# A bound sent ahead of Q's relays, deferred products ahead of the weighting passes, and Q features due earlier in a fused attention and gated-MLP kernel

## The chip, the cores and the metric

One core of a Trainium2 chip runs the whole kernel in one launch. The metric is the device time of one execution in microseconds (us); lower is better. Engines are named as in the profile: PE is TensorE's matmul row, PEld its weight loads, DVE is VectorE, ACT is ScalarE, POOL is GpSimd, SP is SyncE, which here only issues DMAs. PSUM is the accumulator memory that PE writes.

## The reference

`xn` is the layer norm of `x` (2048 rows of 640). Two branches read it, and their results are combined:

```python
xn = _layernorm(x)
s = attention(xn)                       # below
g = silu((sigmoid(xn @ w_gate) * (xn @ w_up)) @ w_down)      # inner width 1536
out = x + s * g

# attention: 32 heads of 20, four segments of 512 rows, q/k/v = xn @ wq/wk/wv
for s in range(4):
    p = softmax(qs @ ks.T * scale + causal_mask)
    a_dot = p @ vs
    pq = phi(qs)                        # phi(t) = t+1 if t > 0 else exp(t)
    a_mem = (pq @ M) / (pq @ z + 1e-6)
    o = sigmoid(beta) * a_mem + (1 - sigmoid(beta)) * a_dot
    M, z = M + phi(ks).T @ vs, z + sum(phi(ks))
s = concat(o) @ wo
```

So each segment of 512 rows does causal softmax attention within itself, and reads a running memory `M` of the segments before it through the features `phi(q)`.

## The kernel before, in words

**Slots.** After a prologue the program is written out as 80 slots, 20 in each of the four segments. A slot handles one unit of the causal scores: four heads at a time, five units to a pair of head groups, four pairs to a segment. Slot `s` begins with `scores` (L516): four or eight groups of small matmuls into the one PSUM tile `Sps` (L522), then one 2048-wide exponential on ACT into `pt` (L527), then the causal cut on POOL (L530). One or two slots later `weigh` (L534) multiplies `pt` with V into the PSUM tile `Aps` (L547). When a head group is complete (after unit 2's first part and unit 4), `weigh` also puts three DVE instructions in line: the reciprocal `rd` (L553), its scaling (L554) and the product `od` (L556). `Aps` is single-buffered, so the next head group's first `weigh` waits for that `od`.

**What fills the slots.** All other work is put between `scores` calls by a planner. Its pieces are the next segment's projections (`v_tile` L360, `k_chunk` L289, `q_chunk` L321), the MLP (`gate` L428, `up` L438, `down` L456), the output projection (`o_proj` L502), the memory's update and reading (`m_update` L388, `mem_read` L410), loads and stores. `at(time, cost, ...)` gives a piece a due time in slots; the constant `R` = 20/24 scales the times in the text, so that `R * 18.3` is 15.25 slots after the segment's start. There are three heaps: `tasks` (PE work with a cost), `soft` (everything without), and `first` (only `phi`). The MLP's pieces stand in a list `bulk`, taken at a rate that evens out the slots' planned PE cost: a slot that has less fixed cost gets more of `bulk`. Within a slot the order is: `scores`; `fill` with `tasks` due before the slot's 0.45; the due `weigh` calls; `flush`; `phi` pieces due in this slot; `fill` with everything else due in it. `later(lag, ...)` puts the next step of a piece `lag * R` slots on.

**Deferred products.** `up` and `down` end in a DVE product (`hT` L442, `aa` L461) that frees one of only three PSUM buffers of the pool `d`, which all projections, MLP pieces and the bound share. The first part of each slot runs with `delay[0] = True`: these products are then kept in `pending` and issued by the `flush` behind the `weigh` calls, or sooner if the buffer is needed.

**Q, its bound and its features.** The scores need, beside Q, a bound on each score row so that the exponentials stay in range. Q's projection `q_chunk(n, c)` (five chunks) is copied to `q5`, with absolute values in `aq` (L324). `q_bound` (L329) multiplies `aq` with per-head column maxima of K (`cps`, L334), and ACT copies it to `cb` (L337). Q and bound then go out to DRAM and come back in the layout of `scores`, all through SP's one queue: `stage_out` writes `q5` (`Qs`, L310), `relay` reads it back as four DMAs (`QT<-Qs`, L274), `c_out` writes `cb` (`Cs`, L345), `c_in` reads it back as four DMAs per half into other rows of the same tiles (`QT<-Cs`, L353). Each half has its own `QT` tile. SP issues in program order and stops at a DMA whose wait isn't over.

`phi(n, "q5", c)` later overwrites `q5` with the features: an exponential on ACT into one of three `ex` buffers (L370; `cb` takes its buffer from the same three), and 0.8 R later two DVE instructions `rest` (L373, L374) in place, which must wait until the DMA to `Qs` has read the chunk. Only `mem_read` of the next segment's slots reads them.

**Prologue.** For segment 0 the same steps are written out by hand in `startup`. Behind Q's last chunk come `relay(0, 0, Qs, QT)`, `q_bound(0)`, the second half of Q, `c_in(0, (0,))`, then the loads of the second third of the MLP weights (`load_glu(1, 0)` and `(1, 1)`, L163: `Wg1`, `Wu1`), and the transposing DMAs of segment 1's `xn` (L263). PE meanwhile runs the eight first MLP pieces (`take`), then slot 0.

Of the kernel before, what the change touches and what calls it, by code (L numbers as in the profile page):

```python
# [55 lines left out]
R = NSLOT / 24  # L56
# [3 lines left out]
def kernel(  # L60
# [42 lines left out]
    def at(time, cost, fn, *a):  # L103
        count[0] += 1
        heapq.heappush(first if fn is phi else tasks if cost > 0.1 else soft, (time, count[0], cost, fn, a))
# [4 lines left out]
    def flush(keep=0):  # L110
        while len(pending) > keep:
            pending.pop(0)[1]()

    def dtile(shape, dtype, name):
        seq[0] += 1
        while pending and pending[0][0] <= seq[0] - 3:
            pending.pop(0)[1]()
        return ps_d.tile(shape, dtype, name=name, tag="d")
# [6 lines left out]
    def later(lag, fn, *a):  # L125
        at(clock[0] + lag * R, 0.0, fn, *a)
# [65 lines left out]
    def v_ones(a, b):  # L192
        for i in range(a, b):
            nc.gpsimd.memset(V[i][:, :, DH:VW], 1.0)
# [73 lines left out]
    def half_tile(tiles, n, half):  # L268
        return tiles[(2 * n + half) % 3]

    def relay(n, half, src, dst):
        rows = src[n % 2].rearrange("(g r d) n -> r d g n", r=4, d=DH)
        for r in range(4):
            nc.sync.dma_start(half_tile(dst, n, half)[32 * r:32 * r + DH, :, :], rows[r][:, 4 * half:4 * half + 4, :])  # L274
# [54 lines left out]
    def q_bound(n):  # L329
        s = st[n]  # L330
        ps = dtile([P, L], F32, "cps")
        for c in range(DC):
            b = c % 4
            nc.tensor.matmul(ps[32 * b:32 * b + H, :], lhsT=s["IK"][:, c, :], rhs=s["aq"][:, c, :],  # L334
                             start=(c < 4), stop=(c not in (0,)), tile_position=(0, 32 * b))
        cb = stg.tile([P, L], BF, name="cb", tag="ex", bufs=3)
        nc.scalar.copy(cb[:], ps[:])  # L337

        if n:
            later(0.8, c_out, n, cb)  # L340
        else:
            c_out(n, cb)

    def c_out(n, cb):
        nc.sync.dma_start(Cs[n % 2].rearrange("b h n -> (b h) n"), cb[:])  # L345
        if n:
            later(1.0, c_in, n)
# [215 lines left out]
    def take(k):  # L563
        for _, fn, a in bulk[:k]:
            fn(*a)
        del bulk[:k]
# [6 lines left out]
    def startup():  # L573
        warm(WARM)
        nc.gpsimd.memset(KT[0][:], 1.0)
        ln_stats(0, 0, 0, 1)
        ln_stats(0, 0, 1, 2)
        ln_norm(0, 0, 0)
        warm(10)
        ln_stats(0, 1, 0, 1)  # L580
        ln_norm(0, 0, 1)
        v_tile(0, 0, 0)
        ln_stats(0, 1, 1, 2)
        v_tile(0, 1, 0)
        ln_norm(0, 1, 0)
        v_tile(0, 0, 1)
        ln_norm(0, 1, 1)
        v_tile(0, 2, 0)
        v_tile(0, 1, 1)
        v_tile(0, 2, 1)  # L590
        v_ones(0, 4)
        make_ind()
        nc.gpsimd.memset(KT[1][:], 1.0)
        for c in range(DC):
            k_chunk(0, c)
        nc.gpsimd.memset(KT[2][:], 1.0)
        stage_out(0, 0, Ks, KT, "k5")
        for c in range(DC):
            q_chunk(0, c)
            if c == 0:  # L600
                stage_out(0, 1, Ks, KT, "k5")
                relay(0, 0, Ks, KT)
            elif c == 2:
                stage_out(0, 0, Qs, QT, "q5")
            if c < 2:
                ln_stats(1, 0, c, c + 1)
        make_bd()
        v_ones(4, 8)
        take(1)
        relay(0, 0, Qs, QT)  # L610
        q_bound(0)
        stage_out(0, 1, Qs, QT, "q5")
        c_in(0, (0,))
        load_glu(1, 0)
        load_glu(1, 1)
        ln_stats(1, 1, 0, 1)
        gates()
        take(1)
        ln_norm(1, 0, 0)
        ln_norm(1, 0, 1)  # L620
        take(1)
        ln_stats(1, 1, 1, 2)
        take(5)
        at(0.1, 0.68, v_tile, 0, 3, 0)
        at(0.5, 0.68, v_tile, 0, 3, 1)
        at(R * 2.0, 0.0, ln_norm, 1, 1, 0)
        at(R * 2.3, 0.0, ln_norm, 1, 1, 1)
        load_glu(2, 0)
        load_glu(2, 1)
        relay(0, 1, Ks, KT)  # L630
        relay(0, 1, Qs, QT)
        c_in(0, (1,))
# [6 lines left out]
    for n in range(NSEG):  # L639
        w = NSLOT * n  # L640
        m = n + 1
        if m < NSEG:
            if n:
                for p in range(2):
                    for i in range(2):
                        at(w + R * (1.4 * p + 0.7 * i - 3.4), 0.1, ln_stats, m, p, i, i + 1)
                        at(w + R * (0.4 + 1.6 * p + 0.4 * i), 0.1, ln_norm, m, p, i)
            for i in range(8):
                at(w + R * (3.5 + (0.6 * i if i < 4 else 2.5 + 0.55 * (i - 4))), 0.68, v_tile, m, i // 2, i % 2)
            for c in range(DC):  # L650
                at(w + R * (8.8 + 1.0 * c), 1.08, k_chunk, m, c)
                at(w + R * (13.8 + 1.1 * c), 1.08, q_chunk, m, c)
                if m + 1 < NSEG:
                    at(w + R * (12.8 + 0.85 * c), 0.0, phi, m, "k5", c)
                at(w + R * (18.3 + 0.8 * c), 0.0, phi, m, "q5", c)
            at(w + R * 19.0, 0.6, q_bound, m)
            if m + 1 < NSEG:
                for p in range(2):
                    at(w + R * (16.1 + p), 0.0, x_load, m + 1, p)
            if n == 0:  # L660
                for c in range(DC):
                    at(R * (2.6 + 0.8 * c), 0.0, phi, 0, "k5", c)
            for i, cs in enumerate(([0, 1, 2], [3, 4])):
                at(w + R * (10.0 + 3.2 * i), 0.75 - 0.25 * i, m_update, n, cs)
        if n >= 1:
            for j in range(4):
                at(w + R * (1.1 + 0.3 * j), 0.0, o_ready, n - 1, j)
                at(w + R * (4.0 + 0.5 * j if j < 3 else 9.6), 0.0, xr_load, n - 1, j)
            for i in range(8):
                at(w + R * (5.4 + 1.1 * i), 0.68, o_proj, n - 1, i // 2, i % 2)  # L670
                at(w + R * (3.4 + 0.85 * i), 0.25, mem_read, n, i // 2, i % 2)
# [17 lines left out]
    for n in range(NSEG):  # L689
        st[n]["od"] = opool.tile([P, 4, D], BF, name="od")  # L690
        if n:
            bulk += [(1.09, fn, (n, f)) for f in range(FC) for fn in (gate, up)]
        bulk += [(1.64, down, (n, j, h)) for j in range(4) for h in range(2)]
        keep = 4 if n >= NSEG - 2 else 0

        left = sum(b[0] for b in bulk[:len(bulk) - keep])
        fixed = [PASS[i % NU] + sum(t[2] for t in tasks if i <= t[0] - NSLOT * n < i + 1) for i in range(NSLOT)]
        level = min(fixed)
        while sum(max(level - f, 0.0) for f in fixed) < left:
            level += 0.01  # L700
        given, goal = 0.0, 0.0

        def fill(until, heaps):
            nonlocal given
            while True:
                ready = [h for h in heaps if h and h[0][0] < until]
                if ready:
                    run_task(min(ready, key=lambda h: h[0][:2]))
                if len(bulk) > keep and given + 0.5 * bulk[0][0] <= goal:
                    cost, fn, a = bulk.pop(0)  # L710
                    given += cost
                    fn(*a)
                elif not ready:
                    break

        for slot in range(NSLOT):
            pair, u = divmod(slot, NU)
            now = NSLOT * n + slot
            share = max(level - fixed[slot], 0.0)
            pt = scores(n, pair, u)  # L720
            delay[0] = True
            goal += FIRST * share
            fill(now + 0.45, (tasks,))
            for w in due:
                weigh(*w)
            delay[0] = False
            flush()
            while first and first[0][0] < now + 1.0:
                run_task(first)
            due, held = held, []  # L730
            due.append((n, pair, u, UNITS[u][0][0], pt))
            if u == 2:
                held.append((n, pair, u, 1, pt))
            goal += (1.0 - FIRST) * share
            fill(now + 1.0, (tasks, soft))
        while len(bulk) > keep:
            cost, fn, a = bulk.pop(0)
            fn(*a)
# [47 lines left out]
```

## Time and profile before

| what | value |
|---|---|
| median of 3 runs | 340.95 us (340.71 to 341.32) |
| the profiled execution | 342.2 us, of which its span is 340.5 us |
| PE busy | 330.1 us, 97% of the span |
| DVE, ACT busy | 223.6 and 225.7 us, 66% each |
| POOL busy | 111.5 us, 33% |
| granted TensorE clock | full in every fortieth of the span |
| chain that ended last | PE 83%, DMA 6%, DVE 6%, ACT 2% |

The span is what the profile shows from its first to its last instruction; 1.7 us of that execution lie around it. The shares are of busy time over the whole span. The first 40 us (prologue) and the last 15 us differ from the middle. PE's row merges pipelined matmuls, so that its busy time also holds short gaps between instructions.

### The profile page before, as it was taken

Reading aid. Unit: us, or ns where it says so; the run is one execution under the profiler, and the core shown is the slowest. Engines: PE = TensorE matmul, PEld = TensorE weight load, DVE = VectorE, ACT = ScalarE, POOL = GpSimd, SP = SyncE. Lnnn points to the kernel's source line nnn. Section 1 sums busy time; section 2 is a strip of 40 time slices with the busy share of each in tenths; the row PEclk is TensorE's granted clock in tenths of the full one; section 3 lists DMA queues with packets and bytes.
Section 4 is the critical chain, followed back from the end, with each engine's and each line's share of the span. In section 5 each row is a group of like instructions: output and inputs, shape, how many; then the busy total and the mean of one; then the engine's idle time right before and its main releaser. Section 6 shows DMA issues by size and latency. Waiting matters only on the chain.

```text
span 340.5 us, 8352 instructions
## 1 busy us (share of the span) xinstructions
PE 330.1 (97%) x3402; PEld 186.8 (55%) x3402; DVE 223.6 (66%) x533; ACT 225.7 (66%) x236; POOL 111.5 (33%) x157
## 2 busy tenths in 40 slices
PE   8999899999999999999999999999999999999995
PEld 7543455545664565554466456554456655544673
DVE  6375366769786577778758867885655677633455
ACT  3652797688886666477686765565887775786730
POOL 6645232222245222332235312323222323233214
PEclk9999999999999999999999999999999999999999
DMA  7953984665822621045720461042220521110032
GB/s 237 339 182 108 329 130 87 229 212 125 185 74 37 120 74 45 19 137 93 218 72 2 87 127 40 21 154 80 79 69 3 84 74 40 58 60 2 3 62 77
DMA packets 54725, 35.53 MB, mean 104 GB/s; under 512 B 28576, under 2 KB 54688, under 8 KB 54688
## 3 DMA queue, kind: packets, MB, share of 16 engines
q1 hardware_dynamic: 52480, 32.23, 36.5%
q10 hardware_dynamic: 2208, 2.79, 2.5%
q8 instruction: 26, 0.43, 0.5%
q14 instruction: 11, 0.09, 0.1%
HBM read 20.19 MB, written 8.39 MB: 84 GB/s over the span
## 4 chain that ended last, share of the span: by engine, by line
PE 83%; DMA 6%; DVE 6%; ACT 2%; POOL 1%; issue 1%; SPq 1%; DVEq 0%; ACTq 0%; POOLq 0%
PE up L438 14%; PE gp L428 14%; PE yp L456 11%; PE Aps L547 8%; PE Sps L522 6%; PE psk L289 6%; PE sp L502 6%; PE psv L360 6%; PE psq L321 6%; DMA Cs<-cb 2%; DMA Wu<-in_B_w_up_dram 2%; PE wps L571 2%; DMA xnT<-xn 1%; PE dm L388 1%; DMA Qs<-q 1%; PE am L410 1%
## 5 line engine op out<-in xcount | busy, mean ns | idle before, releaser
L527 ACT ACTIVATE pt<-Sps 128x2048 bf16<-128x2048 f32 x80 | 150.2, 1877 | 28.9 <-PE Sps L522 26.1
L530 POOL TENSOR_SCALAR_AFFINE_SELECT pt<-pt 128x1024 bf16<-128x1024 bf16 (+1 forms) x80 | 75.7, 947 | 196.7 <-ACT pt L527 196.7
L428 PE MATMUL gp<-xnT,Wg 128*128 128x512 bf16 x240 | 59.7, 379 | 1.1 <-DMA Wg<-in_B_w_gate_dram 0.6
L438 PE MATMUL up<-xnT,Wu 128*128 128x512 bf16 x240 | 59.7, 380 | 0.2 <-DMA Wu<-in_B_w_up_dram 0.2
L456 PE MATMUL yp<-Wd,hT 128*128 128x320 bf16 x384 | 57.1, 299 | 0.0
L442 DVE SCALAR_TENSOR_TENSOR hT<-tg,up 128x512 bf16<-128x512 bf16 x48 | 32.7, 682 | 30.4 <-PE up L438 27.4
L431 ACT ACTIVATE tg<-gp 128x512 bf16<-128x512 f32 x48 | 28.6, 597 | 35.9 <-PE gp L428 35.9
L547 PEld LDWEIGHTS <-pt 128*128 128x128 bf16 x1280 | 43.3, 96 | 14.7 <-DVE od L556 1.4
L547 PE MATMUL Aps<-va,pt 128*128 128x21 bf16 x1280 | 44.6, 173 | 0.9 <-DVE od L556 0.7
L456 PEld LDWEIGHTS <-hT 128*128 128x128 bf16 x384 | 35.3, 97 | 15.3 <-issue 2.4
L438 PEld LDWEIGHTS <-Wu 128*128 128x128 bf16 x240 | 21.2, 97 | 24.6 <-issue 3.5
L522 PE MATMUL Sps<-QT,KT 24*128 24x128 bf16 (+3 forms) x512 | 32.6, 301 | 1.4 <-ACT pt L527 0.7
L428 PEld LDWEIGHTS <-Wg 128*128 128x128 bf16 x240 | 21.0, 97 | 22.9 <-issue 2.1
L461 DVE SCALAR_TENSOR_TENSOR aa<-t,yp 128x320 bf16<-128x320 bf16 x32 | 15.2, 482 | 19.5 <-ACT t L459 19.3
L360 PE MATMUL psv<-Wv,xnT 128*128 128x320 bf16 x160 | 26.4, 300 | 0.8 <-ACT tg L431 0.5
L459 ACT ACTIVATE t<-yp 128x320 bf16<-128x320 f32 x32 | 14.0, 437 | 19.2 <-PE yp L456 18.0
L502 PE MATMUL sp<-Wo,oT 128*128 128x320 bf16 x160 | 25.9, 300 | 0.0
L522 PEld LDWEIGHTS <-KT 24*128 24x128 bf16 x512 | 9.5, 92 | 27.0 <-issue 25.9
L321 PE MATMUL psq<-xnT,Wq 128*128 128x512 bf16 x100 | 24.3, 380 | 0.0
L289 PE MATMUL psk<-xnT,Wk 128*128 128x512 bf16 x100 | 24.3, 380 | 0.0
L504 DVE SCALAR_TENSOR_TENSOR aa<-aa,sp 128x320 bf16<-128x320 bf16 x32 | 15.5, 485 | 8.5 <-PE sp L502 8.4
L553 DVE RECIPROCAL rd<-Aps 128x16 f32<-128x16 f32 x32 | 8.1, 254 | 16.4 <-PE Aps L547 16.4
(74 smaller groups left out, 333.6 us busy)
## 6 DMA issues: line engine op xcount, KB each, us to landing
KT<-Ks SPq DMA_DIRECT2D x32, 80.0 KB
QT<-Qs SPq DMA_DIRECT2D x32, 80.0 KB
xr<-in_A_x_dram SPq DMA_DIRECT2D x15, 160.0 KB
out_dram<-xr SPq DMA_DIRECT2D x15, 160.0 KB
xt<-in_A_x_dram SPq DMA_DIRECT2D x6, 320.0 KB
Wg<-in_B_w_gate_dram SPq DMA_DIRECT2D x3, 640.0 KB
Wu<-in_B_w_up_dram SPq DMA_DIRECT2D x3, 640.0 KB
Wd<-in_B_w_down_dram ACTq DMA_DIRECT2D x1, 1920.0 KB
```

The costliest lines, as they stand in the source:

```text
L289: nc.tensor.matmul(ps[:], lhsT=W["k"][:, k, c * P:(c + 1) * P], rhs=s["xnT"][:, k, :], start=(k == 0), stop=(k == DC - 1))
L321: nc.tensor.matmul(ps[:], lhsT=W["q"][:, k, c * P:(c + 1) * P], rhs=s["xnT"][:, k, :], start=(k == 0), stop=(k == DC - 1))
L360: nc.tensor.matmul(ps[:], lhsT=s["xnT"][:, k, j * P:(j + 1) * P], rhs=W["v"][:, k, half * HB:(half + 1) * HB], start=(k == 0), stop=(k == ...
L428: nc.tensor.matmul(gp[:], lhsT=Wg[f // 4][:, k, fo:fo + P], rhs=s["xnT"][:, k, :], start=(k == 0), stop=(k == DC - 1))
L438: nc.tensor.matmul(ps[:], lhsT=Wu[f // 4][:, k, fo:fo + P], rhs=s["xnT"][:, k, :], start=(k == 0), stop=(k == DC - 1))
L442: empty(lambda: nc.vector.scalar_tensor_tensor(out=h[:], in0=tg[:], scalar=1.0, in1=ps[:], op0=ALU.add, op1=ALU.mult))
L456: nc.tensor.matmul(yp[:], lhsT=s["hT"][f][:, j * P:(j + 1) * P], rhs=W["d"][:, f, hs], start=(f == 0), stop=(f == FC - 1))
L502: nc.tensor.matmul(sp[:], lhsT=s["oT"][:, j, c, :], rhs=W["o"][:, c, hs], start=(c == 0), stop=(c == DC - 1))
L522: nc.tensor.matmul(Sps[:, r, c0:c0 + ncol], lhsT=kt[32 * r:32 * r + KR, gi, kb * P:(kb + 1) * P], rhs=qt[32 * r:32 * r + KR, gi, kb * P:L] ...
L527: nc.scalar.activation(pt[:], Sps[:], ACT.Exp, scale=SCALE)
L530: nc.gpsimd.affine_select(out=diag, in_=diag, compare_op=ALU.is_ge, fill=0.0, base=0, pattern=[[0, 4], [0, cnt], [1, P]], channel_multipli ...
L547: nc.tensor.matmul(A[:, qb, r, :], lhsT=pt[:, r, off:off + P], rhs=V[4 * (n % 2) + kb][:, 4 * g + r, :], start=first, stop=True, skip_grou ...
```

## The change

Three places move, and nothing is added or removed: every instruction of before is issued again, in another order.

1. In `startup`, `q_bound(0)`, with its write of `cb` to DRAM, stands ahead of `relay(0, 0, Qs, QT)`.
2. In the segments, the five `phi(m, "q5", c)` are due from `R * 17.4` on (14.50 slots) where it was `R * 18.3` (15.25), and `q_bound(m)` at `R * 19.2` (16.0) where it was `R * 19.0` (15.83).
3. In each slot `flush()` stands ahead of the `weigh` calls where it stood behind them.

```diff
@@ startup
         take(1)
+        q_bound(0)
         relay(0, 0, Qs, QT)
-        q_bound(0)
         stage_out(0, 1, Qs, QT, "q5")
         c_in(0, (0,))
@@ segment plan
-                at(w + R * (18.3 + 0.8 * c), 0.0, phi, m, "q5", c)
-            at(w + R * 19.0, 0.6, q_bound, m)
+                at(w + R * (17.4 + 0.8 * c), 0.0, phi, m, "q5", c)
+            at(w + R * 19.2, 0.6, q_bound, m)
@@ each slot
             fill(now + 0.45, (tasks,))
+            flush()
             for w in due:
                 weigh(*w)
             delay[0] = False
-            flush()
             while first and first[0][0] < now + 1.0:
                 run_task(first)
```

## The prediction

> **What bounds the kernel now.** The page's first part comes first, then PE's waits.
>
> ```profile
> PE 330.1 (97%) x3402; PEld 186.8 (55%) x3402; DVE 223.6 (66%) x533; ACT 225.7 (66%) x236; POOL 111.5 (33%) x157
> ```
>
> Of PE's own waits, two lines are for loads:
>
> ```profile
> PE gp L428 <- DMA Wg<-in_B_w_gate_dram: 0.6, 1, 0.6
> PE up L438 <- DMA Wu<-in_B_w_up_dram: 0.2, 1, 0.2
> ```
>
> PE is the bound, with 10.4 us (340.5 - 330.1) not busy, part of it at start and end. The change leaves PE's work as it is, so it can act only on PE's pauses. The timeline of the prologue shows the largest one:
>
> ```profile
> 23.00 0.39 SPq L310 DMA_DIRECT2D Qs<-q  x1
> 25.03 0.58 ACT L337 CAST cb<-cps 128x512 bf16<-128x512 f32 x1
> 26.35 1.43 SPq L274 DMA_DIRECT2D QT<-Qs  x4
> 27.88 0.35 SPq L345 DMA_DIRECT2D Cs<-cb  x1
> 28.27 0.43 SPq L310 DMA_DIRECT2D Qs<-q  x1
> 30.86 1.28 SPq L353 DMA_DIRECT2D QT<-Cs  x4
> 32.19 0.39 SPq L163 DMA_DIRECT2D Wg<-in_B_w_gate_dram  x1
> 32.62 0.52 SPq L163 DMA_DIRECT2D Wu<-in_B_w_up_dram  x1
> 33.51 1.00 PE L522 MATMUL Sps<-QT,KT 24*128 24x512 bf16 x3 [0.36 <-DMA QT<-Cs]
> 36.58 1.25 PE L428 MATMUL gp<-xnT,Wg 128*128 128x512 bf16 x5 [0.60 <-DMA Wg<-in_B_w_gate_dram]
> 38.38 1.25 PE L438 MATMUL up<-xnT,Wu 128*128 128x512 bf16 x5 [0.22 <-DMA Wu<-in_B_w_up_dram]
> ```
>
> The bound is in `cb` at 25.61, but SP stands at Q's relay until `Qs` has landed (26.35), issues four relays, and reaches the bound's write at 27.88. The bound's reading follows its landing at 30.86, the MLP weights at 32.19. PE began its first scores at 32.58 and is through with them at 34.44 (in the middle such a group costs 0.33, 41.05 to 41.38): its row counts most of this stall as busy. Then it waits for `Wg1` and `Wu1`.
>
> Other pauses, in the timeline of the segments (a slot begins where PE loads its scores' first weights: slot 15 at 84.30, 17 at 91.15, 19 at 99.66, 28 at 134.86, 36 at 168.78, 65 at 275.81):
>
> ```profile
> 91.66 0.40 PE L522 MATMUL Sps<-QT,KT 24*128 24x256 bf16 x8 [0.43 <-ACT pt L527]
> 100.73 0.76 PE L547 MATMUL Aps<-va,pt 128*128 128x21 bf16 x24 [0.67 <-DVE od L556]
> 141.54 0.67 PEld L547 LDWEIGHTS <-pt 128*128 128x128 bf16 x24 [0.47 <-DVE od L556]
> 167.29 0.38 PE L334 MATMUL cps<-aq,IK 128*32 128x512 bf16 x1 [0.39 <-DVE aq L324]
> 280.14 1.24 PE L428 MATMUL gp<-xnT,Wg 128*128 128x512 bf16 x5 [0.38 <-DVE hT L442]
> ```
>
> The reader sees three owners: scores or bound near slots 15 to 17 and 35, the next weighing behind `od`, an MLP piece whose PSUM buffer a deferred product still holds.
>
> **Part 1, the prologue.** PE, ACT and DVE keep their order; SP's changes. The bound's write goes out at about 25.7, while SP would wait for `Qs` anyway, so the relays stay at 26.35 to 27.78. The cover is 0.7 us (25.61 to 26.35); were `cb` later than that, the relays and all behind them would be later by the same. `Qs`'s second half follows at 27.9 to 28.3 (0.35 sooner). The bound took 2.97 us from issue to its reader's issue, so it is there at 25.7 + 2.97 = 28.65, and `c_in` starts then: 2.2 us sooner. `Wg1`, `Wu1`, the transposes of `xn` and the rest of the queue move by the same 2.2.
>
> SP also holds back a DMA until the one eight places ahead of it has landed: among the waits from 36 to 48 us stand
>
> ```profile
> SPq L274 <- DMA Wu<-in_B_w_up_dram: 2.6, 1, 2.6
> SPq L274 <- DMA Wg<-in_B_w_gate_dram: 2.0, 1, 2.0
> ```
>
> and the third and fourth of those Q relays are eight DMAs behind `Wg2` and `Wu2`, which they don't read. In the new order `c_in`'s fourth DMA (29.7) is eight behind the first relay (26.35), `Wg1` behind the second: 3.3 us, where the bound's own trip took 2.97, so no wait, but with little to spare.
>
> PE's chain without waits from 32.58: scores 0.33, two V tiles 1.54 (34.44 to 35.98), gate 1.18 (36.58 to 37.76), scores and issue 0.40 (37.76 to 38.38, less the wait), so `up` at 36.03 where it was 38.38: at most 2.35 sooner. `Wu1` landed at 38.34; 2.2 sooner is 36.14. The load decides, and the gain is **2.2**. From 34 to 46 us the DMA share is near 1, but from 30 to 34 it is 0.21 and 0.27, so an earlier load uses idle engines. The next hard point, `xnT` at 52.2 (PEld waits 0.43), comes down the same queue and moves along.
>
> By the Trainium skill (DMA: Bandwidth & Descriptors, "Queues, rings and completion order") each DMA engine takes its descriptors in ring order, so `c_in` stands behind the data of the relays and of `Qs`'s second half, however early it is issued. The trace agrees that this data flows until about 30.7 (the bound, queued among it, landed at 30.84). That is the first rival.
>
> **Part 2, features and bound.** Worked out from the due times: the features' exponentials of chunks 0, 1, 2, 3, 4 fall into slots 14, 15, 15, 16, 17 of the segment (before 15, 15, 16, 17, 17); their `rest` into 15, 15, 16, 17, 17 (before 15, 16, 17, 17, 18). `q_bound` goes from the end of slot 15 to just behind slot 16's scores, and 0.6 of planned MLP work moves the other way: in segment 1 `up` changes places with the bound, in segment 2 likewise; in segment 0 only the bound moves. SP's order stays.
>
> *Segment 0 to 1.* Slot 17's scores waited 0.43, because slot 16's exponential started at 89.72 behind two features and `cb`. Now `cb` is behind it, and the wait goes: -0.43. Does the first feature start sooner? `rest` of chunk 0 started at 89.88, when `Qs` (85.61 + 4.17) had landed: it stands in DVE's queue earlier, but starts where it did, and `aa` behind it has its tanh only at 91.93. So this half of the change does not do what it says here. `cb` comes at about 91.7, when SP reaches it anyway (91.78).
>
> *Segment 1 to 2.* The bound waited 0.39 for `aq`, in front of slot 36's scores. Behind them it doesn't: -0.4 (bounds: 0, and -0.99, the idle PEld after it). `cb` then comes about 3 us later (behind a 1.88 exponential), the bound's reading at about 175 instead of 173.96; slot 40 needs it at 185.18. Segment 2 to 3: no wait before, 0 (bounds +-0.4, a switch of matmul shape, PEld's 0.42 of "issue"); its reading moves from 248.1 to about 250.5, and slot 60 begins at 260.22.
>
> **Part 3, `flush` first.** It changes DVE's order in 15 slots, where a head group ends and a product is pending. There `hT` (0.68) or `aa` (0.49) goes ahead of `rd`, `rd`, `od`. Between `od`'s end and the next weighing lie 0.06 (slots 18, 28), 0.55 (78), 0.59 (68), 0.60 (60), 0.82 (38), and over 1.1 in the other nine, which cover either product.
> - Slot 18: DVE is behind its work (the third feature ends at 99.77), `aa` adds 0.49. The tanh ahead comes 0.42 sooner, since one feature less stands on ACT, and DVE catches up by that: `od` ends 0.07 later. But PE arrives 0.43 sooner, so it waits 0.5 longer: **+0.5**, which takes back segment 0's 0.43.
> - Slot 28: `hT` goes ahead of `rd` at 140.20: +0.68 at most, +0.35 if the scaling, which took 0.48, takes the 0.18 it takes elsewhere: **+0.5**.
> - Slots 38, 60, 68: covered. Slot 78: the tanh ends at 319.84, then `aa` 0.49 and 0.98 for the three: 321.35, where PE arrives at 321.35: +0.1 (to +0.3).
> - Slot 65, the gain: `hT` (279.41) goes ahead of `rd` (278.50), and the gate at 280.14 loses its wait: **-0.4**.
>
> **Sum:** -2.2 - 0.43 - 0.4 + 0.5 + 0.5 + 0.1 - 0.4 = -2.3. The profiled execution took 342.2 (span 340.5, 1.7 around it), which makes 339.9; the median of the runs is 1.25 lower, which gives 340.95 - 2.3 = **338.6**. Its own range, from the bounds (part 1 -1.8 to -2.4, part 2 0 to -1.4, part 3 +0.2 to +1.2): 337.6 to 339.4.
>
> **Rivals.**
> 1. *The bound's reading is served late.* If the relays' and `Qs`'s data until 30.7 go first, `c_in` transfers from there; it took up to 3.5 us from 30.86 to 34.4. Scores would be through at about 33.5 to 34.2, and `Wg1` comes 1 to 1.5 sooner instead of 2.2: total -1.2, 339.7. For: its trip is long for 64 KB. Against: the bound's own 128 KB leave that stretch. If `c_in` also waits for the relays' landing, 340.2. The ring order of the skill's page would give the 339.7.
> 2. *No change:* PE gets to its next fixed point, `xnT` at 52.2 or a pending load, and waits there, as the transfers end when they did. Then only parts 2 and 3 are left: -0.1, 340.85. For: DMA share near 1 from 34 to 46. Against: the idle 30 to 34.
> 3. *Slower:* DVE stands at a deferred `aa` whose tanh is stuck on ACT behind a 1.88 exponential, with `rd`, `rd`, `od` queued behind it and PE's next weighing behind them. It is possible where the product is `down`'s (slots 15, 18, 38, 60, 78), and decides where the tanh ends later than the weighing by more than the slack. Against: the tanh ended only 0.1 (slot 15: 88.32 to 88.23) to 0.4 later (slot 78: 319.84 to 319.44). Were three slots to pay 1.3 (1.88 less 0.6 of slack) beyond the sum, 338.6 + 3.9 = 342.5.
>
> **Chances.** Forecast 0.60; late service 0.17 (mostly still faster); no change 0.12; slower 0.11. About 0.2% (0.7 us) can be told from no change here. So: faster 0.75, within 0.2% 0.14, slower 0.11. The range 337.5 to 340.6 takes in the forecast's own range, the late service and a little of no change.
>
> **What would show it.** Right: `Cs` near 25.7 and `c_in` near 28.6 with the relays still at 26.35; the first scores done by 33.0; `up` on `Wu1` near 36.1; no wait of slot 17's scores nor of the second bound; longer waits on `od` in slots 19 and 29 (about 1.2 and 1.0), none on `hT` in slot 66. Wrong: `c_in` still after 30, slot 0's scores still waiting past 33.5, a new wait for `xnT`, or waits on `od` in slots other than these two.

## The result, and the profile after

The changed kernel takes 339.38 us (median of 18 runs, 338.38 to 342.29) where the kernel before took 341.24 (18 runs on the same chip). The ratio is 0.9945 with an interval of 0.9921 to 0.9969: faster by 1.9 us, with an interval of 1.1 to 2.7. The profiled execution took 339.46, with a span of 337.7; its total is a typical one. The page's first part:

```profile
PE 325.5 (96%) x3360; PEld 186.2 (55%) x3402; DVE 224.5 (66%) x533; ACT 225.8 (67%) x236; POOL 110.8 (33%) x157
```

DVE, ACT and POOL are as before. PE's busy time is 4.6 lower without any work taken away: 42 fewer matmuls are in the record, and the stall of the first scores, which counted as busy, is gone. The timeline of the prologue, with the columns start, duration, engine, line, instruction, and in brackets the wait and its releaser:

```profile
21.86 0.39 SPq L310 DMA_DIRECT2D Qs<-q  x1
25.03 0.58 ACT L337 CAST cb<-cps 128x512 bf16<-128x512 f32 x1
25.64 0.35 SPq L345 DMA_DIRECT2D Cs<-cb  x1
26.04 1.53 SPq L274 DMA_DIRECT2D QT<-Qs  x4
27.61 0.38 SPq L310 DMA_DIRECT2D Qs<-q  x1
28.09 1.46 SPq L353 DMA_DIRECT2D QT<-Cs  x4
29.59 0.40 SPq L163 DMA_DIRECT2D Wg<-in_B_w_gate_dram  x1
32.59 0.46 PE L522 MATMUL Sps<-QT,KT 24*128 24x512 bf16 x4
36.23 1.25 PE L438 MATMUL up<-xnT,Wu 128*128 128x512 bf16 x5 [0.24 <-DMA Wu<-in_B_w_up_dram]
```

The bound's write goes out at 25.64, as soon as `cb` is there, the relays right behind it, and the bound's reading at 28.09 instead of 30.86. SP's own waits show a change of owner: before, SP stood 2.1 us for the bound to land in `Cs`; now it comes to the reading only after five more DMAs and has no wait for `Cs`, here and in the three other traces with this order. The first scores run without a wait and are through at 33.05, and `up` on `Wu1` starts 2.15 sooner. PE's waits further on, in the list of waits of after (total, times, longest):

```profile
PE Aps L547 <- DVE od L556: 2.5, 2, 2.1
PE Sps L522 <- ACT pt L527: 0.5, 2, 0.3
PE up L438 <- DMA Wu<-in_B_w_up_dram: 0.2, 1, 0.2
```

Four entries of before are gone: `gp` on `Wg`, `psv` on `tg`, `cps` on `aq`, `gp` on `hT`. One has grown, the weighing's wait for `od`, from 0.7 to 2.5. The timeline shows where:

```profile
88.88 1.16 POOL L530 TENSOR_SCALAR_AFFINE_SELECT pt<-pt 128x1024 bf16<-128x1024 bf16 x1 [3.43 <-ACT pt L527]
88.99 0.58 ACT L337 CAST cb<-cps 128x512 bf16<-128x512 f32 x1 [0.17 <-DVE q L374]
89.11 1.46 DVE L374 SCALAR_TENSOR_TENSOR q<-ex,q 128x512 bf16<-128x512 bf16 x1
90.67 0.63 ACT L370 ACTIVATE ex<-q 128x512 bf16<-128x512 bf16 x1 [0.76 <-DVE q L374]
93.42 0.49 DVE L461 SCALAR_TENSOR_TENSOR aa<-t,yp 128x320 bf16<-128x320 bf16 x1 [1.52 <-ACT t L459]
99.51 0.76 PE L547 MATMUL Aps<-va,pt 128*128 128x21 bf16 x24 [2.10 <-DVE od L556]
140.37 0.76 PE L547 MATMUL Aps<-va,pt 128*128 128x21 bf16 x24 [0.44 <-DVE od L556]
260.50 0.40 PE L522 MATMUL Sps<-QT,KT 24*128 24x128 bf16 x8 [0.27 <-ACT pt L527]
```

Slot 19's wait (99.51) grew from 0.67 to 2.10, slot 29's (140.37) is 0.44, where before only the weight loads beside it waited, 0.47 (now 0.77), and slot 61's scores (260.50) wait 0.27 where before had nothing.

What each slot gave or took is read from the start of its first score weight load, less the same of before. This lead is the measure used below; minus is sooner. What a slot gives or takes is its change from this slot's start to the next one's, good to about 0.02 us. Up to slot 6 PE still waits for loads of the prologue, 0.2 to 0.7 us for `Wu1` and up to 0.4 for `xnT`, differently from trace to trace; so the middle is counted from slot 6 on.

| kernel | lead at slot 1 | at slot 6 | at slot 79 | gained behind slot 6 |
|---|---|---|---|---|
| after | -2.17 | -2.31 | -2.74 | -0.43 |
| part 1 alone | -1.35 | -1.49 | -1.50 | -0.01 |
| part 2 alone | -1.29 | -1.44 | -1.39 | +0.05 |
| part 3 alone | -1.17 | -0.63 | -1.38 | -0.75 |
| features sooner alone | -1.37 | -1.54 | -1.02 | +0.52 |
| bound later alone | -0.80 | -0.88 | -1.71 | -0.83 |
| one flush (slot 43) alone | -1.16 | -1.00 | -1.62 | -0.62 |
| all parts, `cb` out of the ring | -1.76 | -1.39 | -3.25 | -1.86 |
| the best version | -1.73 | -1.54 | -4.00 | -2.46 |

The first column holds the main surprise: kernels whose prologue is that of before reach slot 1 by 0.80 to 1.37 sooner than the profiled execution of before did.

### The profile page after: what moved, and what is told of

Its sections match the earlier page's. It is cut to its first block, busy times and chain, and to the rows that moved or that the text cites. A ratio compares the mean times of both kernels' runs of the same rounds, so it can differ in the third digit from the quotient of the medians.

```text
span 337.7 us, 8319 instructions
## 1 busy us (share of the span) xinstructions
PE 325.5 (96%) x3360; PEld 186.2 (55%) x3402; DVE 224.5 (66%) x533; ACT 225.8 (67%) x236; POOL 110.8 (33%) x157
## 4 chain that ended last, share of the span: by engine, by line
PE 82%; DVE 7%; DMA 4%; ACT 2%; issue 2%; SPq 1%; POOL 0%; DVEq 0%; ACTq 0%
PE up L438 14%; PE gp L428 14%; PE yp L456 11%; PE Aps L547 9%; PE Sps L522 7%; PE sp L502 6%; PE psv L360 6%; PE psk L289 6%; PE psq L321 6%; DMA Wu<-in_B_w_up_dram 2%; DMA Qs<-q 1%; ACT pt L527 1%; PE dm L388 1%; PE am L410 1%; DVE q L374 1%
## 5 line engine op out<-in xcount | busy, mean ns | idle before, releaser
L438 PE MATMUL up<-xnT,Wu 128*128 128x512 bf16 x229 | 58.8, 379 | 0.8 <-DMA Wu<-in_B_w_up_dram 0.2
L428 PE MATMUL gp<-xnT,Wg 128*128 128x512 bf16 x221 | 58.0, 379 | 1.2 <-issue 0.2
L442 DVE SCALAR_TENSOR_TENSOR hT<-tg,up 128x512 bf16<-128x512 bf16 x48 | 32.7, 682 | 35.0 <-PE up L438 30.3
L522 PE MATMUL Sps<-QT,KT 24*128 24x128 bf16 (+3 forms) x512 | 31.8, 301 | 0.9 <-ACT pt L527 0.5
L461 DVE SCALAR_TENSOR_TENSOR aa<-t,yp 128x320 bf16<-128x320 bf16 x32 | 15.4, 481 | 23.3 <-ACT t L459 23.2
L321 PE MATMUL psq<-xnT,Wq 128*128 128x512 bf16 x96 | 23.6, 380 | 0.6 <-issue 0.5
L289 PE MATMUL psk<-xnT,Wk 128*128 128x512 bf16 x92 | 23.5, 380 | 0.3
L502 PEld LDWEIGHTS <-oT 128*128 128x128 bf16 x160 | 14.5, 98 | 8.1 <-issue 2.0
```

What stands on the lines that cost most here:

```text
L289: nc.tensor.matmul(ps[:], lhsT=W["k"][:, k, c * P:(c + 1) * P], rhs=s["xnT"][:, k, :], start=(k == 0), stop=(k == DC - 1))
L321: nc.tensor.matmul(ps[:], lhsT=W["q"][:, k, c * P:(c + 1) * P], rhs=s["xnT"][:, k, :], start=(k == 0), stop=(k == DC - 1))
L428: nc.tensor.matmul(gp[:], lhsT=Wg[f // 4][:, k, fo:fo + P], rhs=s["xnT"][:, k, :], start=(k == 0), stop=(k == DC - 1))
L438: nc.tensor.matmul(ps[:], lhsT=Wu[f // 4][:, k, fo:fo + P], rhs=s["xnT"][:, k, :], start=(k == 0), stop=(k == DC - 1))
L442: empty(lambda: nc.vector.scalar_tensor_tensor(out=h[:], in0=tg[:], scalar=1.0, in1=ps[:], op0=ALU.add, op1=ALU.mult))
L502: nc.tensor.matmul(sp[:], lhsT=s["oT"][:, j, c, :], rhs=W["o"][:, c, hs], start=(c == 0), stop=(c == DC - 1))
```

## The experiments

All times below are medians against runs of the kernel before on the same chip (341.40 for the first four kernels, 341.31 for the others).

### Part 1 alone

```
@@ startup
         take(1)
+        q_bound(0)
         relay(0, 0, Qs, QT)
-        q_bound(0)
```

> Only part 1 (the bound's write ahead of Q's relays in the prologue). Account read from the two traces: slot 1's scores start 2.2 us sooner than before, slot 6's 2.3, and every later slot the same 2.3, so the time is 2.3 us (0.7%) below the kernel before. Rival: the gain is given back at a load or another wait in the first 60 us or at a later segment's start; then the slots' lead shrinks on the way and the time is less than 1 us below.

Measured: 340.72 us, ratio 0.9976 (0.9956 to 0.9995), so -0.8 with an interval of -1.5 to -0.2. The timeline has the order of after, and a later end:

```profile
23.58 0.39 SPq L310 DMA_DIRECT2D Qs<-q  x1
25.97 0.35 SPq L345 DMA_DIRECT2D Cs<-cb  x1
28.76 1.44 SPq L353 DMA_DIRECT2D QT<-Cs  x4
37.06 1.25 PE L438 MATMUL up<-xnT,Wu 128*128 128x512 bf16 x5 [0.25 <-DMA Wu<-in_B_w_up_dram]
```

Behind slot 6 the lead doesn't change (-1.49 to -1.50): what this part gives is decided in the prologue and kept to the end, so the rival "no change" is out. But the gain is 0.8 where 2.2 was forecast, and neither the account above (2.3) nor its rival (a lead that shrinks on the way) came.

### Part 2 alone, and why part 1 is worth 0.8

```
@@ segment plan
-                at(w + R * (18.3 + 0.8 * c), 0.0, phi, m, "q5", c)
-            at(w + R * 19.0, 0.6, q_bound, m)
+                at(w + R * (17.4 + 0.8 * c), 0.0, phi, m, "q5", c)
+            at(w + R * 19.2, 0.6, q_bound, m)
```

> Only part 2 (features due sooner, bound later). Account: the scores of slot 17 lose their wait (-0.5) and segment 1 gains about 0.7 at slots 35 to 36, but the third ex buffer in line is now chunk 1's, so ACT waits for that chunk's rest, the tanh, DVE and od come late, and PE's wait on od in slot 19 grows from 0.67 to about 1.6 without any help of the flush: in sum -0.2 us. Rival, the account of the prediction: slot 19's wait is the flush's doing, and here it is no more than 1.1; in sum -0.8 us.

Measured: 340.51 us, ratio 0.9979 (0.9956 to 1.0002): not told apart from no change. Its timeline, with the prologue of before and slot 19:

```profile
21.95 0.39 SPq L310 DMA_DIRECT2D Qs<-q  x1
29.38 1.39 SPq L353 DMA_DIRECT2D QT<-Cs  x4
37.13 1.25 PE L438 MATMUL up<-xnT,Wu 128*128 128x512 bf16 x5 [0.26 <-DMA Wu<-in_B_w_up_dram]
...
99.97 0.76 PE L547 MATMUL Aps<-va,pt 128*128 128x21 bf16 x24 [1.70 <-DVE od L556]
```

This is the old order, in which `Qs` was issued at 23.00, `c_in` at 30.86 and `up` at 38.38 in the profile of before. Here the same instructions come at 21.95, 29.38 and 37.13. Six traces have the old prologue: `up` on `Wu1` at 38.38, 37.13, 37.46, 37.06, 37.65 and 37.47, mean 37.53. Four have the new one: 36.23, 37.06, 37.12 and 36.72, mean 36.78. The means differ by 0.75, which is the 0.8 that the times gave. The largest difference of any pair, 38.38 to 36.23, is the pair that the two profiled executions happened to be.

The same ten traces show a second loss. `Wu1`'s load is issued at 31.65 on the mean of the six and at 30.34 on the mean of the four, 1.31 sooner. But from its issue to `up`'s start it takes 5.76 to 6.09 us in the old order and 6.20 to 6.66 in the new one, 0.57 more on the mean, so that 0.75 of the 1.31 is left. Why the earlier load takes longer is not shown.

In the middle, slot 17 gives 0.49, slots 35 and 36 together 0.67 and slot 20 0.26; slots 18, 19 and 61 take 0.14, 1.03 and 0.28. No flush is moved here, and slot 19's wait for `od` is 1.70 all the same: most of its growth belongs to part 2.

### Part 3 alone

```
@@ each slot
             fill(now + 0.45, (tasks,))
+            flush()
             for w in due:
                 weigh(*w)
             delay[0] = False
-            flush()
```

> Only part 3 (flush ahead of the weighing). Account: slot 43's V tile no longer waits (-0.6, because the product hT that frees its PSUM buffer is issued 2 us sooner), the gate of slot 66 neither (-0.45), against +0.5 in slot 19 and +0.2 in slot 29, perhaps +0.3 in slot 61: in sum -0.2 us. Rival, the account of the prediction: the V tile of slot 43 waited for ACT's tanh as the profile names it, so nothing is gained there, and slot 29 pays 0.5: in sum +0.7 us.

Measured: 340.45 us, ratio 0.9977 (0.9957 to 0.9998), so -0.8. Slot 19 in its timeline:

```profile
100.50 0.76 PE L547 MATMUL Aps<-va,pt 128*128 128x21 bf16 x24 [1.07 <-DVE od L556]
```

By slots: +0.40 in 19 (0.26 of it given back in the next), +0.22 in 29, -0.49 in 66, and -0.68 in 43, which the prediction didn't have. The flush's +0.40 and part 2's +1.03 in slot 19 make 1.43; the whole change has 1.42. So the two losses add up and don't depend on each other.

### The bound out of the ring of exponentials

All three parts, and `cb` stands in a chunk of `aq`, which the bound's matmuls have just read, instead of one of the three `ex` buffers:

```
-        cb = stg.tile([P, L], BF, name="cb", tag="ex", bufs=3)
-        nc.scalar.copy(cb[:], ps[:])
+        cb = s["aq"][:, 0, :]
+        nc.scalar.copy(cb, ps[:])
```

> The changed kernel with cb written into the first chunk of aq, so that it takes none of the three ex buffers. Account (the ring of ex buffers makes slot 19's wait): chunk 3's exponential no longer waits for chunk 1's rest (0.76 in the changed kernel), slot 17's exponential starts about 1 us sooner against its scores, PE's wait on od in slot 19 falls from 2.10 to about 1.0, and the time is about 1 us below the changed kernel, 3.5 to 3.8 below the one before. Rival (chunk 1's rest, which took 1.46 us instead of 0.7, and DVE's load are the cause): the wait stays at 1.8 or more and the time is the changed kernel's.

Measured: 338.46 us, ratio 0.9918 (0.9892 to 0.9944), so -2.8, where 3.5 to 3.8 was expected. The timeline at the same place as after's above:

```profile
89.80 1.12 POOL L530 TENSOR_SCALAR_AFFINE_SELECT pt<-pt 128x1024 bf16<-128x1024 bf16 x1 [3.43 <-ACT pt L527]
90.00 1.46 DVE L374 SCALAR_TENSOR_TENSOR q<-ex,q 128x512 bf16<-128x512 bf16 x1
90.42 0.65 ACT L370 ACTIVATE ex<-q 128x512 bf16<-128x512 bf16 x1
93.19 0.49 DVE L461 SCALAR_TENSOR_TENSOR aa<-t,yp 128x320 bf16<-128x320 bf16 x1 [0.40 <-ACT t L459]
99.28 0.77 PE L547 MATMUL Aps<-va,pt 128*128 128x21 bf16 x24 [1.10 <-DVE od L556]
```

In after, `cb` took the buffer of chunk 0, so that the exponential of chunk 3 had to wait for the buffer of chunk 1, that is for its `rest`, which took 1.46. Here `rest` takes 1.46 too, but the exponential of chunk 3 doesn't wait for it; the tanh behind it isn't late (`aa` waits 0.40, not 1.52), and slot 19's wait falls from 2.10 to 1.10. Slot 19 costs 0.43, about what the flush alone costs there (0.40). Two rivals are out: it isn't the stretched `rest` by itself, and it isn't the flush. Slot 61's 0.28 is gone too.

### Features sooner alone, and the bound later alone

The two edits of part 2, each by itself:

```
-                at(w + R * (18.3 + 0.8 * c), 0.0, phi, m, "q5", c)
+                at(w + R * (17.4 + 0.8 * c), 0.0, phi, m, "q5", c)
```

> Only the features due sooner, the bound where it was. Account (the ring of three ex buffers decides): three exponentials now stand ahead of cb on ACT, so cb's buffer is chunk 0's, which is free only after that chunk's rest, about 1 us after Qs has landed; cb stands ahead of slot 16's exponential, so slot 17's scores wait about 1.5 us more than before (0.43), and the time from slot 16 to slot 20 grows by 1 us or more: slower than the kernel before by 1 us over the segments, the prologue's share aside. Rival: the features' times don't matter by themselves; slots 16 to 20 stay within 0.3 us of before.

Measured: 343.30 us, ratio 1.0062 (1.0036 to 1.0089): slower by 2.1.

```profile
89.16 0.59 ACT L337 CAST cb<-cps 128x512 bf16<-128x512 f32 x1 [1.34 <-DVE q L374]
89.64 1.88 ACT L527 ACTIVATE pt<-Sps 128x2048 bf16<-128x2048 f32 x1
91.57 0.40 PE L522 MATMUL Sps<-QT,KT 24*128 24x256 bf16 x8 [1.89 <-ACT pt L527]
```

The same ring, now in front of the path: `cb` stands ahead of slot 16's exponential and waits 1.34 for chunk 0's `rest`, the exponential is late, and slot 17's scores wait 1.89 instead of 0.43. Slot 17 takes 1.45; slot 20 gives 0.26 and slot 35 gives 0.66. That makes 0.52 lost behind slot 6 in all. This execution took 341.17, the fastest of ten, so what the others lose beyond that isn't seen.

```
-            at(w + R * 19.0, 0.6, q_bound, m)
+            at(w + R * 19.2, 0.6, q_bound, m)
```

> Only the bound later, the features where they were. Account: the two gains of part 2 are the bound's alone: slot 17's scores wait no longer (-0.5), and slots 35 to 36 get 0.7 shorter; without the features' move chunk 1's rest doesn't fall beside POOL's cut (0.7 us, not 1.46) and slot 19's wait on od grows by what PE is ahead, from 0.67 to about 1.1. From slot 15 to the end 0.7 us less than before. Rival (both moves are needed): no more than 0.2 less.

Measured: 340.51 us, ratio 0.9974 (0.9949 to 0.9998), so -0.9.

```profile
99.39 0.76 PE L547 MATMUL Aps<-va,pt 128*128 128x21 bf16 x24 [0.70 <-DVE od L556]
```

Slot 17 (-0.49) and slots 35 and 36 (-0.67) give all that they give in the whole change; slot 19 loses nothing (its wait is 0.70, where 1.1 was expected), slot 61 loses 0.28. So the bound's edit needs no help from the features for these gains, and slot 17's is its alone. The gain near slot 35 comes with either edit: with the features alone `up` also stands ahead of the bound there (166.08 and 167.25), the wait for `aq` is gone, and both edits together give no more than one. What the features give beyond that is slot 20's 0.26. They don't start much sooner themselves: their first `rest` starts at 87.86 in after, when `Qs` has landed, as it did at 89.88 before: 2.0 sooner, where the slots themselves were 2.3 sooner.

### One flush alone

The flush goes first in slot 43 and nowhere else:

```
+            if now == 43:
+                flush()
             for w in due:
                 weigh(*w)
             delay[0] = False
             flush()
```

> The kernel before with the flush ahead of the weighing in slot 43 alone, one product hT put ahead of rd, rd, od. Account: slot 43's last V tile waits for the PSUM buffer which that hT frees, though the profile of before names ACT's tanh; so slot 43 gets 0.68 us shorter and no other slot changes. Rival (the tanh, as the profile names it): slot 43 stays as it was, to 0.1 us.

Measured: 340.74 us, ratio 0.9984 (0.9962 to 1.0006): too small for the times. In the trace slot 43 gives 0.68, slot 44 takes 0.08, and no other slot changes behind slot 6. The timeline of before, of this place:

```profile
199.68 0.60 ACT L431 ACTIVATE tg<-gp 128x512 bf16<-128x512 f32 x1 [1.20 <-PE gp L428]
199.70 0.68 DVE L442 SCALAR_TENSOR_TENSOR hT<-tg,up 128x512 bf16<-128x512 bf16 x1
200.33 0.84 PE L360 MATMUL psv<-Wv,xnT 128*128 128x320 bf16 x5 [0.52 <-ACT tg L431]
```

and of the experiment:

```profile
197.47 0.69 DVE L442 SCALAR_TENSOR_TENSOR hT<-tg,up 128x512 bf16<-128x512 bf16 x1 [0.65 <-PE up L438]
198.64 0.84 PE L360 MATMUL psv<-Wv,xnT 128*128 128x320 bf16 x5
198.68 0.60 ACT L431 ACTIVATE tg<-gp 128x512 bf16<-128x512 f32 x1 [1.20 <-PE gp L428]
```

The profile of before named the tanh `tg` as the releaser of the V tile. In the experiment the V tile starts 0.04 ahead of that tanh, without a wait. What held it was the product `hT`, which ended 0.10 after the tanh and, by the profile, 0.05 after the V tile's start, and which gives back the PSUM buffer that the V tile takes.

### The best version

From these: parts 1 and 2, `cb` in `aq`, and the flush first only in slots 43 and 65, where it gains.

```
+            if now in (43, 65):
+                flush()
             for w in due:
                 weigh(*w)
             delay[0] = False
             flush()
```

> Parts 1 and 2 whole, cb in aq's first chunk, and the flush ahead of the weighing only in slots 43 and 65, where it freed a buffer that PE waited for. Account: the wait on od in slot 19 falls to about 0.6, as no aa stands ahead of rd there, slot 29 stays at its old 0.47, and the gains of slots 43 and 66 remain: from slot 6 to the end 2.6 us less than before, the prologue about 0.9 less, in sum about 3.5, 0.7 below the kernel with cb in aq and the flush everywhere. Rival (the other flushes help by freeing buffers elsewhere): no faster than that kernel.

Measured: 338.20 us, ratio 0.9903 (0.9876 to 0.9929), so -3.3: faster than the kernel before. Against the changed kernel (0.9945) and the one with `cb` in `aq` and every flush first (0.9918) its ratio is lower too, but the intervals meet, so that the times do not rule out its rival; in the traces it gains 2.03 and 0.60 more behind slot 6.

```profile
98.73 0.76 PE L547 MATMUL Aps<-va,pt 128*128 128x21 bf16 x24 [0.70 <-DVE od L556]
```

Slot 19's wait is back to that of before, slot 29 and slot 61 lose nothing. The 2.46 gained behind slot 6 and part 1's 0.8 make 3.3, which is what the times say.

## Why the prediction was right or wrong, step by step

The forecast was 338.6 (-2.3); measured was -1.9. That the total is near is partly luck: part 1 was sized too large, and in the middle a gain and a loss were both missed. The range, too, isn't what its bounds add up to: they give 337.4 to 340.4, not 337.6 to 339.4. The measured 339.38 lies in both.

- **Part 1, the mechanism: right in the order, not in the last wait.** `Cs` went out at 25.64 (25.7 forecast), and the bound's reading and all behind it moved forward. But `c_in` does not hang on the bound's trip of 2.97: SP came to it 2.45 after the bound's issue, with four relays and a store issued in between, and did not wait. So `c_in` started at 28.09, not 28.65. `up` on `Wu1` started at 36.23 where 36.1 was forecast, which is partly luck: the load was issued sooner than forecast and took longer (6.20 from its issue to `up`'s start, 5.76 before). The rival "served late" did not come for the first scores: they were through at 33.05, where it had 33.5 to 34.2. The order of the rings that the Trainium skill states (DMA: Bandwidth & Descriptors, "Queues, rings and completion order") was no limit for them; no run shows whether it held.
- **Part 1, the size: wrong, -2.2 for about -0.8.** This is the largest error. The main failed step is the sum's base: the prediction saw that the profiled execution was 1.25 above the median and took this off at the end, and at the same time priced the stall from that execution. The other five traces with the old prologue have `up` on `Wu1` 1.03 sooner on the mean, so most of the 1.25 was in the very stall that the change takes away, and it was counted twice. The other is that the loads were to move along by the same 2.2: issued 1.31 sooner on the mean, they served `up` only 0.75 sooner. What the new order takes away is shown best by the trace of part 1 alone. There `Qs` was issued at 23.58, later than the 23.00 of before, and SP waited 0.5 for it ahead of the relays; yet `c_in` came at 28.76, not 30.86, because `Cs` was already out. That a late `Qs` makes every slow prologue of the old order was not tried.
- **Part 2, slot 17 and segment 1: right, one too small.** -0.49 (forecast -0.43) and -0.67 (forecast -0.4, with bounds 0 and -0.99), between the bounds; that a part of the weight load's idle time went along is likely, not shown. Segment 2 to 3 took 0.55 in slot 55 and gave 0.54 in the next, so 0, as forecast.
- **Part 2, the ring: missed.** The step "`cb` is behind it, and the wait goes" followed `cb` in ACT's order and didn't ask which `ex` buffer it takes. It takes chunk 0's, the exponential of chunk 3 then needs chunk 1's, and with `rest` stretched to 1.46 beside POOL this made 1.03 in slot 19. Slot 61's 0.28 was missed too. It comes with the bound later and goes with `cb` out of the ring; how one leads to the other is open.
- **Part 3, slot 18 to 19: right for the flush.** +0.40 alone (forecast +0.5); 1.42 with the ring's share.
- **Part 3, slot 28 to 29: too large.** +0.22 for +0.5. Slots 38, 60, 68 and 78 lost nothing, so rival 3, an `aa` stuck behind an exponential, didn't come in the slots named for it. Slot 19 was its pattern (`aa` waits 1.52 for its tanh), but with the ring as the cause and in the features' place, not the flush's.
- **Part 3, slot 65 to 66: right.** -0.49 for -0.4.
- **Part 3, slot 43: missed, -0.68.** The prediction looked for pieces whose wait names `hT`, and found one. The other names the tanh `tg`, because the V tile waits for several things and tanh and product end together.

By the traces the middle gave -0.43, where the forecast had -0.1. With part 1's 0.8 this makes -1.2, and the times say -1.9 (-1.1 to -2.7). After and part 2 alone, the two kernels with the collision in the ring, came out 0.7 better in the times than in their one trace, which is still within their intervals; the times of the bound, of part 3, and of the best version agree with theirs within 0.1. The features alone came out 1.6 worse than in their trace, and much of that goes with the clock: five of its ten executions were granted 0.994 or 0.995 and took 344.3 on the mean, the five at 1.0 took 342.5. That is 1.0 above the kernel before at 0.999 or more (341.5), where the trace has 0.52. Whether the ring's price differs between executions is open.

## What to carry to other kernels

Before pricing a stall from one profiled execution, ask whether that execution's excess over the median lies in that stall; a chain of DMAs through DRAM is the first place to look, and the price of the stall and the excess must not both be counted. Nor does a load that is issued sooner land sooner by as much: here 1.31 became 0.75. When a piece is moved past others that share a ring of buffers with it, follow the ring as well as the engine's order: whose buffer does each now take, and when is that free? And where a wait names an instruction that ends at the same moment as another that frees a buffer, treat both as candidates: here the one not named was the owner.

## What the runs showed of the hardware that was not expected

**The same chain of DMAs differs by over 1 us between executions.** With an identical prologue `c_in` was issued between 29.38 and 30.86, and `up` on `Wu1` started between 37.06 and 38.38.

**DVE's `rest` stretches beside POOL's cut, but products out of PSUM don't.** L374 reads two operands in SBUF; it takes 0.69 alone, and 1.46 to 1.56 where the cut on POOL began before it (after: cut 88.88 to 90.04, `rest` 89.11 to 90.57; twice more, at 168.85 with 1.56 and at 245.5 with 1.46). L442 and L461 have one operand in PSUM; in each of the ten traces 12 to 16 `hT` and 9 to 13 `aa` run beside a cut for at least 0.3 us, and none took over 0.69 and 0.49. Where `rest` began first, at 89.37 in the best version, it took 0.69, and the cut, begun at 89.64, took 1.38; most cuts of this size take 1.10. The Trainium skill (SBUF — State Buffer, "Who interferes with whom") says that a DVE instruction with two SBUF inputs contends with a GpSimd instruction that reads SBUF, that one with at most one SBUF input outside the 2-port modes doesn't, and that issue order decides who blocks. These rows agree. The one that came second was not held back wholly: `rest` ends 0.53 after the cut, sooner than a whole 0.69. In slot 19 the stretch cost next to nothing by itself: with `cb` out of the ring it was still 1.46, and the slot took 0.43, where the flush alone, without a stretch, took 0.40.
